# Attention and ReLU² layer on one core: the first batch's values are scaled by spread reciprocals instead of P, and the order is searched anew

## The chip, the cores and the metric

One Trainium2 chip, one of its cores. The metric is the device time of one execution in microseconds (us), median of several runs; less is better. The core has TensorE for matmuls (PE in the profile, PEld for its weight loads), VectorE (DVE), ScalarE (ACT), GpSimd (POOL), and SyncE (SP), whose queue issues the DMAs here.

## What is computed

Causal attention of 4 batches, 12 heads, 448 positions and head dimension 64, its output laid out as 1792 rows of 768, then two matrix products with a squared ReLU between them:

```python
scores = scale * np.matmul(q, k.transpose(0, 1, 3, 2))
scores = np.where(mask, -1000000000.0, scores)
scores = scores - np.max(scores, axis=-1, keepdims=True)
attn = np.exp(scores)
attn = attn / (np.sum(attn, axis=-1, keepdims=True) + 1e-09)
attn_out = np.matmul(attn, v)
x = attn_out.transpose(0, 2, 1, 3).reshape(B * S, H * D)
g = np.maximum(x @ w_in, 0.0) ** 2        # w_in 768 x 2048
out = g @ w_out                           # w_out 2048 x 768
```

All inputs and outputs are fp32. q and k are drawn with a spread of 0.8, v with 0.1.

## The kernel before

Most products run on pairs of fp16 halves: a value is scaled by a power of two and split into an upper half (its rounding to fp16) and a lower half (the rest), and a product is the sum of three fp16 matmuls. The attention of the first batch is the exception. It is done in fp32, because it runs at the very start, while the weights are still being loaded, narrowed to fp32 words, measured (gram matmuls, L1044 and L1093) and split into halves.

`early(part)` computes that first batch, part 0 for positions 0 to 255 and part 1 for positions 256 to 447. Six pairs of heads are worked through in each part. For one pair, `scored` loads nothing itself; it

- turns Q and K by TensorE transposes (L863) and copies them back (L650),
- multiplies them into scores (L884), one PSUM bank for each head and row block,
- masks them and takes the row maxima on DVE (L892), and
- takes exponentials on ACT into P, which also gives the row sums (L896).

`applied` then takes the reciprocals of the row sums on DVE (L906, L909), multiplies each of the four blocks of P by them (`scaled`, L642, on ACT, DVE or GpSimd), turns the blocks of P by TensorE transposes (L924), copies them back (L650), multiplies them with V (L940), and writes the two fp16 halves of x, both read from PSUM: the upper by `activation` or `tensor_scalar` (L953), the lower by `scalar_tensor_tensor` (L957).

After the first part, phase "n" runs the two layers of the first batch (first layer L1250 in groups of 18 matmuls, second layer L1268 in groups of 6, both at lines that later batches share), while the second half of the weights is still being prepared. The second batch's attention begins with transposes at L718 and scores at L773 and L742. The later batches follow, attention of one beside the layers of another; the last block's first layer is a seven-product scheme (L1357, L1472, L1480).

What sets the order: every operation goes into a plan with the engines that may run it, a cost on each, what it reads and writes, and a due time. The due time is a line of the table `PR` (a start and a step for each phase) plus an offset for each kind of operation; another set of entries biases the choice of engine. `Plan.order` goes through the operations with its own clock and puts them on each engine in order of due time among those that are ready by that clock. The result is one fixed instruction order for each engine, and the chip runs each engine's instructions in it, waiting on semaphores.

## Time and profile before

| | |
|---|---|
| median of 3 runs (lowest to highest) | 628.33 us (627.64 to 629.38) |
| the profiled execution: time, span of its instructions | 626.06 us, 624.3 us |
| granted TensorE clock, mean | 0.999 |
| busy share PE, PEld, DVE, ACT, POOL | 96%, 71%, 80%, 74%, 9% |

The profile shows one execution. "Busy" is the time in which at least one instruction of an engine runs. An idle time is put down to what released the waiting instruction. Matmuls overlap in PE's pipeline, so PE's busy time holds some time in which it only waits for a matmul to drain. POOL does almost nothing in the first 160 us.

### The profile page before, as it was taken

What the parts mean: (1) busy time and instruction counts of PE and PEld (TensorE: products, weight loads), DVE (VectorE), ACT (ScalarE), POOL (GpSimd) and SP (SyncE); (2) the same over time, 40 slices, a digit from 0 to 9 for tenths busy, and PEclk for the clock granted to TensorE, in tenths of its full rate; (3) what the DMA queues carried; (4) which work ended last, traced back from release to release, by engine and by line L of the source; (5) the groups of instructions that cost most, each with busy time, mean ns of one, the idle gap of its engine ahead of it and who ended that gap; (6) DMA issues with size and microseconds to landing.
All of it is one profiled execution on the core that took longest, in us unless ns stands there. A gap on an engine that the chain in (4) does not pass through costs nothing.

```text
span 624.3 us, 14273 instructions
## 1 busy us (share of the span) xinstructions
PE 597.0 (96%) x5178; PEld 440.8 (71%) x5178; DVE 501.6 (80%) x1506; ACT 462.0 (74%) x1332; POOL 53.1 (9%) x93
## 2 busy tenths in 40 slices
PE   6788999989999999999999999999999999899997
PEld 4555778878656577886677767887768776687664
DVE  3899999999776899888899889688996999984100
ACT  4989999888998689868999789898647175584000
POOL 0000000000366000000000224132000000000000
PEclk9999999999999999999999999999999999999999
DMA  9974574665657967928997787865500000000100
GB/s 215 351 225 121 169 264 168 227 205 152 145 140 183 208 121 175 168 66 162 214 220 153 136 207 174 165 122 118 132 29 3 27 11 4 1 2 13 39 26 25
DMA packets 190342, 82.52 MB, mean 132 GB/s; under 512 B 177728, under 2 KB 185152, under 8 KB 190272
## 3 DMA queue, kind: packets, MB, share of 16 engines
q1 hardware_dynamic: 190272, 81.62, 53.1%
q8 instruction: 40, 0.66, 0.4%
q14 instruction: 30, 0.25, 0.1%
HBM read 47.19 MB, written 5.51 MB: 84 GB/s over the span
## 4 chain that ended last, share of the span: by engine, by line
PE 59%; DVE 24%; ACT 9%; DMA 5%; issue 2%; SPq 0%; ACTq 0%; DVEq 0%
PE bank L1268 28%; PE bank L1250 15%; PE bank L1472 5%; PE bank L802 4%; PE bank L759 4%; DVE pq L1357 3%; DMA vn<-in_v_dram 3%; DVE wi L1007 2%; DVE bank L892 2%; DVE wi L1004 2%; DVE g L487 1%; DVE wi L1001 1%; PE bank L773 1%; ACT wo L479 1%; DVE bank L742 1%
## 5 line engine op out<-in xcount | busy, mean ns | idle before, releaser
L1268 PE MATMUL bank<-wo,g 128*128 128x384 f16 x1056 | 183.4, 326 | 1.4 <-DVE ob L1285 0.7
L1250 PE MATMUL bank<-xt,wi 128*128 128x256 f16 (+1 forms) x1728 | 168.9, 255 | 1.7 <-ACT r L1213 1.5
L1250 PEld LDWEIGHTS <-wi 128*128 128x128 f16 x1728 | 144.3, 98 | 19.7 <-issue 3.6
L1268 PEld LDWEIGHTS <-g 128*128 128x128 f16 x1056 | 101.5, 98 | 64.4 <-issue 3.0
L746 ACT ACTIVATE pq<-bank,nm 112x112 f32<-112x112 f32 (+3 forms) x144 | 69.8, 493 | 8.4 <-DVE nm L742 7.2
L479 ACT ACTIVATE psrc<-pq,nm 112x336 f16<-112x336 f32 (+3 forms) x144 | 65.9, 526 | 3.7 <-DMA pt<-psrc 1.8
L492 DVE SCALAR_TENSOR_TENSOR psrc<-pq,nm,psrc 112x336 f16<-112x336 f32 (+3 forms) x120 | 59.8, 528 | 3.4 <-ACT psrc L479 2.7
L1285 DVE SCALAR_TENSOR_TENSOR ob<-bank,fac,ob 128x384 f32<-128x384 f32 x26 | 16.0, 614 | 47.5 <-PE bank L1268 47.5
L742 DVE CUSTOM_DVE_ANT_0 bank<-bank,mask,sc 112x112 f32<-112x112 f32 (+3 forms) x96 | 46.2, 512 | 8.1 <-PE bank L759 3.7
L1280 ACT ACTIVATE ob<-bank,fac 128x384 f32<-128x384 f32 x26 | 15.0, 575 | 47.5 <-PE bank L1268 43.8
L487 DVE TENSOR_TENSOR g<-g,g 128x256 f16<-128x256 f32 (+1 forms) x96 | 38.7, 419 | 10.5 <-ACT g L479 10.2
L1220 ACT ACTIVATE g<-r 128x256 f32<-128x256 f32 (+1 forms) x96 | 34.7, 377 | 8.8 <-DVE r L1215 4.0
L479 ACT ACTIVATE g<-g 128x256 f16<-128x256 f32 (+1 forms) x96 | 35.6, 393 | 0.6
L1472 PEld LDWEIGHTS <-wi 128*128 128x128 f16 x288 | 28.2, 98 | 7.2 <-issue 3.4
L759 PE MATMUL bank<-qk 128*112 128x112 f16 (+3 forms) x192 | 31.5, 284 | 0.0
L802 PE MATMUL bank<-pt,vp 112*64 112x224 f16 (+3 forms) x504 | 30.9, 268 | 0.0
L802 PEld LDWEIGHTS <-vp 112*64 112x64 f16 x504 | 23.5, 109 | 10.2 <-issue 6.0
L746 ACT ACTIVATION_READ_ACCUMULATOR pq<-bank,nm 112x1 f32 x144 | 29.2, 203 | 0.0
L495 POOL TENSOR_SCALAR raw<-raw,sc 112x512 f32<-112x512 f32 x12 | 10.1, 846 | 199.3 <-ACT qs L479 199.3
L495 POOL TENSOR_SCALAR pq<-pq,nm 112x112 f32<-112x112 f32 (+1 forms) x24 | 11.2, 467 | 168.1 <-ACT psrc L479 167.0
L759 PEld LDWEIGHTS <-qk 128*112 128x112 f16 x192 | 21.3, 130 | 5.2
L892 DVE CUSTOM_DVE_ANT_0 bank<-bank,mask 128x128 f32<-128x128 f32 (+3 forms) x48 | 21.6, 488 | 3.3 <-PE bank L884 2.9
(195 smaller groups left out, 1125.1 us busy)
## 6 DMA issues: line engine op xcount, KB each, us to landing
raw<-in_moe_w_out_dram SPq DMA_DIRECT2D x8, 768.0 KB, 5.4
xt<-in_moe_w_out_dram SPq DMA_DIRECT2D x8, 768.0 KB, 4.3
xt<-in_moe_w_in_dram SPq DMA_DIRECT2D x11, 512.0 KB, 4.7
out_dram<-ob SPq DMA_DIRECT2D x26, 192.0 KB, 2.0
raw<-in_moe_w_in_dram SPq DMA_DIRECT2D x9, 512.0 KB, 5.5
vn<-in_v_dram SPq DMA_DIRECT2D x18, 224.0 KB, 2.7
raw<-in_v_dram SPq DMA_DIRECT2D x18, 224.0 KB, 3.2
raw<-in_q_dram SPq DMA_DIRECT2D x12, 224.0 KB, 3.2
```

The source lines that it names most:

```text
L479: nc.scalar.activation(out=o, in_=i, func=ACTF.Copy, scale=s)
L487: return plan.add({"dve": dve_ns(n), "pool": pool2_ns(n)}, lambda e: engines[e].tensor_tensor(out=out(), in0=in_(), in1=top(), op=ALU.subt ...
L492: nc.vector.scalar_tensor_tensor(out=out(), in0=in_(), scalar=scale(), in1=top(), op0=ALU.mult, op1=ALU.subtract)
L742: one("dve", dve_ns(w, 1, 2 if F16S[b] else 1) - 10, lambda e: nc.vector.tensor_tensor_reduce(out=s.ap[0:P, 0:w], in0=s.ap[0:P, 0:w], in1= ...
L746: one("act", act_ns(w, True, 1, True), lambda e: nc.scalar.activation(out=p32[j].ap[0:P, b0 * P:b0 * P + w], in_=s.ap[0:P, 0:w], func=ACTF ...
L759: nc.tensor.matmul(out=s.ap[0:P, 0:(c + 1) * P], lhsT=qT.ap[:, j * NCH + c, :], rhs=kT.ap[:, a:a + c + 1, :].rearrange("p a t -> p (a t)") ...
L802: nc.tensor.matmul(out=pv.ap[j * D:(j + 1) * D, ca * P:t1], lhsT=vp.ap[:, hv, vb:vb + D], rhs=pT[j].ap[0:P, hp * ns + x:hp * ns + x + w, : ...
L892: one("dve", dve_ns(w, 1, 1) - 10, lambda e, c=c, j=j, w=w, ss=ss, nm=nm: nc.vector.tensor_tensor_reduce(out=ss[j].ap[0:M, 0:w], in0=ss[j] ...
L1220: nc.scalar.activation(out=g32.ap[:, 0:n], in_=r.ap[:, 0:n], func=ACTF.Square)
L1250: nc.tensor.matmul(out=h.ap[:, 0:n], lhsT=wi_hl(ci, hw)[:, ms], rhs=x[:, kd, hx, off:off + n], start=(kd == 0 and hw == 0 and hx == 0), st ...
L1268: nc.tensor.matmul(out=o.ap[:, 0:HALF], lhsT=gsl(kf, hg, tt * 128, (tt + 1) * 128), rhs=wo_hl(kf, hw)[:, hh * HALF:(hh + 1) * HALF], start ...
L1472: nc.tensor.matmul(out=ps.ap[:, 0:n], lhsT=A[0](f, kd, hw)[:, ms], rhs=B[0](kd, hx), start=(kd == 0 and hw == 0 and hx == 0), stop=(kd == ...
```

## The change

P is no longer multiplied by the reciprocals. TensorE spreads them instead: four small fp32 matmuls for each pair, with the reciprocals of one row block, read 64 times over, as the weights and the identity as the moving operand, write the reciprocal of each position's row sum into all 64 rows of its head, in the same PSUM bank as the values (columns 256 on). A copy brings them to SBUF; then DVE multiplies the values by them and by the power of two of V into an fp32 tile, the upper half is a plain copy of that tile, and the lower half the tile less the upper half. The space is that of P, whose blocks have been turned by then. The transposes of P wait only for the exponentials now; the reciprocals are needed when the values are multiplied.

```diff
             for j in range(2):
                 due = (phase, 2 * pr + j, "P")
-                for c in range(2):
-                    w = T0 + (c + 1) * M
-                    blk = lambda c=c, j=j, w=w, p32=p32: p32[j].ap[0:M, at[c]:at[c] + w]
-                    scaled(w, blk, blk, lambda c=c, j=j: rr(2 * j + c, 2 * j + c + 1), [(p32[j], c), (nm, "r")], [(p32[j], c)], due)
...
+                for c in range(2):
+                    for j in range(2):
+                        nc.tensor.matmul(
+                            out=pv.ap[j * D:(j + 1) * D, 256 + c * M:256 + (c + 1) * M],
+                            lhsT=rr(2 * j + c, 2 * j + c + 1).to_broadcast([M, D]), rhs=ident[0:M, 0:M],
+                            start=True, stop=True)
...
-            one("pe", (mm32_ns(256) + mm32_ns(128) if part == 0 else 3 * mm32_ns(192) + mm32_ns(96)) + 95, values,
-                [k_ for z in range(part + 1) for k_ in early_keys(2, z, pr)] + [(p_, x) for p_ in pT for x in range(part + 1)],
+            one("pe", (mm32_ns(256) + mm32_ns(128) if part == 0 else 3 * mm32_ns(192) + mm32_ns(96)) + 95 + 2 * mm32_ns(M), values,
+                [(nm, "r")] + [k_ for z in range(part + 1) for k_ in early_keys(2, z, pr)] + [(p_, x) for p_ in pT for x in range(part + 1)],
                 [pv], (phase, 2 * pr + 1, "val"), tiled=True)
...
-            plan.add({"act": act_ns(N, True, 1), "dve": dve_ns(N, 1, 1)}, lambda e, xs=xs, pv=pv:
-                     nc.scalar.activation(out=xs[:, 0], in_=pv.ap[:, 0:N], func=ACTF.Copy, scale=v_up(slot)) if e == "act"
...
-            one("dve", dve_ns(N, 1, 1), lambda e, xs=xs, pv=pv: nc.vector.scalar_tensor_tensor(
-                out=xs[:, 1], in0=pv.ap[:, 0:N], scalar=v_up(slot), in1=xs[:, 0], op0=ALU.mult, op1=ALU.subtract),
-                [pv, ("vup", slot)] + xk, xk, due)
+            y = lambda p32=p32: p32[0].ap[:, 0:N]
+            yk = [(p32[0], 0), (p32[0], 1)]
+            br = lambda p32=p32: p32[1].ap[:, 0:N]
+            bk = [(p32[1], 0), (p32[1], 1)]
+            copy(N, br, lambda pv=pv: pv.ap[:, 256:256 + N], [pv], bk, due)
+            one("dve", dve_ns(N, 1, 1), lambda e, y=y, pv=pv, br=br: nc.vector.scalar_tensor_tensor(
+                out=y(), in0=pv.ap[:, 0:N], scalar=v_up(slot), in1=br(), op0=ALU.mult, op1=ALU.mult),
+                [pv, ("vup", slot)] + bk, yk, due)
+            plan.add({"act": act_ns(N), "dve": dve_ns(N, 2)}, lambda e, xs=xs, y=y:
+                     nc.scalar.activation(out=xs[:, 0], in_=y(), func=ACTF.Copy) if e == "act"
+                     else nc.vector.tensor_copy(out=xs[:, 0], in_=y()), yk, xk, due, "top", True)
+            one("dve", dve_ns(N), lambda e, xs=xs, y=y: nc.vector.tensor_tensor(
+                out=xs[:, 1], in0=y(), in1=xs[:, 0], op=ALU.subtract), yk + xk, xk, due, port=True)
```

All numbers of the table `PR` are replaced as well, for instance:

```diff
-    "B1": -4624022, "B2": -750857, "B3": -6169730, "E0": -10980905, "ER": 294079, "F0": -3639158, "FR": 662526,
+    "B1": -4626895, "B2": -1030135, "B3": -5959485, "E0": -11215955, "ER": 274558, "F0": -4013644, "FR": 598546,
```

What that does to the order, in three places. Line numbers of the changed kernel are 1 higher than before up to the edit in `applied`, 3 less at the transposes of P (L924 becomes L921), and 3 to 8 higher behind them (L940 becomes L943, L1250 becomes L1258). All 48 multiplications of P stood on ACT, and all 12 new copies (L651) and upper halves (L964) stand there too.

ACT at the first two pairs, before: exponentials (L896), the multiplications of P (L642), copies of transposes (L650).

```order
L896 ACTIVATE pq,sm<-bank_107,nm 128x128
L896 ACTIVATE pq,sm<-bank_111,nm 128x128
L642 ACTIVATE pq<-pq,nm 128x128
L642 ACTIVATE pq<-pq,nm 128x256
L642 ACTIVATE pq<-pq,nm 128x128
L642 ACTIVATE pq<-pq,nm 128x256
L896 ACTIVATE pq,sm<-bank_115,nm 128x256
L650 ACTIVATE pt<-bank_127 128x384
L650 ACTIVATE pt<-bank_123 128x384
L896 ACTIVATE pq,sm<-bank_119,nm 128x256
```

The same place in the change, up to the first upper half (L964):

```order
L897 ACTIVATE pq,sm<-bank_107,nm 128x128
L651 ACTIVATE pt<-bank_127 128x384
L651 ACTIVATE pt<-bank_123 128x384
L897 ACTIVATE pq,sm<-bank_111,nm 128x128
L651 ACTIVATE wo<-bank_127 128x2x2x128
L897 ACTIVATE pq,sm<-bank_115,nm 128x256
L897 ACTIVATE pq,sm<-bank_119,nm 128x256
L651 ACTIVATE pq<-bank_103 128x256
L651 ACTIVATE pt<-bank_123 128x384
L964 ACTIVATE xt_142<-pq 128x256
```

The four multiplications between the exponentials of the second pair are gone, and the copy of the spread reciprocals (from bank 103) and the upper half come behind those exponentials.

PE at the first two pairs, before: transposes of P (L924), of the next pair's Q and K (L863), values (L940), scores (L884).

```order
L924 MATMUL bank_127<-ident,pq 128x128 x3
L924 MATMUL bank_123<-ident,pq 128x128 x3
L863 MATMUL bank_127<-ident,wo 128x128 x4
L940 MATMUL bank_103<-pt,wo 64x256 x2
L940 MATMUL bank_103<-pt,wo 64x128 x2
```

In the change:

```order
L921 MATMUL bank_127<-ident,pq 128x128 x3
L921 MATMUL bank_123<-ident,pq 128x128 x3
L885 MATMUL bank_115<-wo 128x256
L885 MATMUL bank_119<-wo 128x256
L864 MATMUL bank_127<-ident,wo 128x128 x4
L935 MATMUL bank_103<-ident,nm 64x128 x4
L943 MATMUL bank_103<-pt,wo 64x256 x2
L943 MATMUL bank_103<-pt,wo 64x128 x2
```

The four spreading matmuls (L935) stand directly ahead of the values, and the transposes have moved ahead of half of the second pair's scores.

PE just ahead of the first product of the first layer (L1250), before: the last early work there is a values group (L940) and scores (L884) of part 1, then gram matmuls (L1044, left out here) and one group of transposes (L924).

```order
L863 MATMUL bank_115<-ident,wo 128x96 x4
L940 MATMUL bank_103<-pt,wo 64x192 x6
L940 MATMUL bank_103<-pt,wo 64x96 x2
L884 MATMUL bank_107<-wo 96x256
L884 MATMUL bank_111<-wo 96x256
L884 MATMUL bank_107<-wo 96x96
L884 MATMUL bank_111<-wo 96x96
...
L924 MATMUL bank_115<-ident,psrc_145 128x96 x4
...
L1250 LDWEIGHTS wi
L1250 MATMUL bank_123<-xt_142,wi 128x256
```

In the change:

```order
L935 MATMUL bank_103<-ident,nm 64x96 x4
L943 MATMUL bank_103<-pt,wo 64x192 x6
L943 MATMUL bank_103<-pt,wo 64x96 x2
L921 MATMUL bank_115<-ident,psrc_146 128x96 x4
...
L921 MATMUL bank_115<-ident,psrc_146 96x96 x3
...
L1024 MATMUL bank_127<-wi,dg 128x512
L1025 LDWEIGHTS minus
L1025 MATMUL bank_127<-wi,minus 128x512
L921 MATMUL bank_115<-ident,psrc_146 128x96 x4
L1258 LDWEIGHTS wi
L1258 MATMUL bank_123<-xt_142,wi 128x256
```

The values group shown there is that of the second pair of part 1, where before it was that of the first. Over all that stands ahead of the first layer's first product, PE has 75 transposes of P instead of 54, 52 score matmuls instead of 44, 40 value matmuls instead of 32, 40 transposes of Q and K instead of 36, 7 of the rest pairs (L1016, L1017) instead of 6, 56 gram matmuls as before, and 32 of the 48 spreading matmuls. Ahead of the second batch's first transposes (L718) there are 60 second-layer matmuls instead of 30 and 96 gram matmuls of w_out instead of 90; the 576 first-layer matmuls of the first batch are all ahead of them in both. SyncE issues the first two loads of w_in ahead of the last two loads of V's second half instead of behind them. From about 255 us of the profile before to the end, PE's and DVE's orders are the same in both kernels but for a few second-layer groups, and upper halves of later batches (L815 on DVE, L814 on ACT): DVE has one of these where it had eight.

## Rows read from the trace of the kernel before

**Rows 1.** The page, part 1: busy time, share of the span, instructions.

```profile
PE 597.0 (96%) x5178; PEld 440.8 (71%) x5178; DVE 501.6 (80%) x1506; ACT 462.0 (74%) x1332; POOL 53.1 (9%) x93
```

**Rows 2.** Windows: busy us (x instructions): PE, PEld, DVE, ACT, POOL; clock; DMA.

```profile
20.00:62.00 42.00, 34.77 (x280) 22.40 (x279) 41.64 (x150) 39.06 (x116) 0.00 (x0) 1.00 0.70 222
62.00:120.00 58.00, 56.85 (x540) 45.70 (x538) 57.83 (x141) 55.79 (x147) 0.00 (x0) 1.00 0.61 206
120.00:155.00 35.00, 32.49 (x446) 28.87 (x444) 33.58 (x82) 27.05 (x86) 0.00 (x0) 1.00 0.60 187
155.00:255.00 100.00, 97.28 (x831) 66.35 (x829) 80.81 (x278) 87.64 (x258) 25.55 (x54) 1.00 0.73 158
255.00:485.00 230.00, 229.90 (x2058) 173.44 (x2056) 196.09 (x623) 187.78 (x560) 26.21 (x30) 1.00 0.66 139
```

**Rows 3.** Windows, 0 to 125 us, of L642 alone.

```profile
0.00:125.00 125.00, 22.82 (x48) 1.00 0.69 218
```

**Rows 4.** Timeline: start, duration, instruction, [idle before it and its releaser].

```profile
9.32 2.74 SPq L834 DMA_DIRECT2D wo<-in_v_dram  x4
...
13.70 1.49 ACT L642 ACTIVATE pq<-pq,nm 128x128 f32<-128x128 f32 x4
...
14.31 0.74 PEld L924 LDWEIGHTS bank<-ident,pq 128*128 128x128 f32 x4 [0.65 <-ACT pq L642]
...
16.95 0.17 DVE L906 TENSOR_SCALAR nm<-sm 128x4 f32<-128x4 f32 x1 [2.03 <-ACT pq L896]
...
17.68 0.43 DVE L1001 TENSOR_SCALAR wi<-g 128x512 int32<-128x512 int32 x1 [0.35 <-DMA g<-in_moe_w_in_dram]
```

**Rows 5.** Groups by form: count, busy us, mean ns of one, idle before.

```profile
L1213 ACT ACTIVATE r<-bank 128x256 f32<-128x256 f32 x32 | 11.7, 381 | 2.3 <-PE bank L1250 1.4 <-PE bank L759 0.9
...
L953 ACT ACTIVATE xt<-bank,vst 128x256 f16<-128x256 f32 x6 | 3.0, 492 | 0.0
...
L479 ACT ACTIVATE xt<-g 128x256 f16<-128x256 f32 x8 | 3.1, 403 | 0.0
...
L957 DVE SCALAR_TENSOR_TENSOR xt<-bank,vst,xt 128x256 f16<-128x256 f32 x6 | 2.8, 465 | 0.0
...
L487 DVE TENSOR_TENSOR xt<-g,xt 128x256 f16<-128x256 f32 x8 | 3.3, 418 | 0.3 <-ACT xt L479 0.3
...
L953 ACT ACTIVATE xt<-bank,vst 128x192 f16<-128x192 f32 x6 | 2.5, 415 | 0.0
```

**Rows 6.** Timeline of PE: two groups of value matmuls.

```profile
21.26 0.87 PE L940 MATMUL bank<-pt,wo 128*64 128x256 f32 x8
...
98.49 1.36 PE L940 MATMUL bank<-pt,wo 128*64 128x192 f32 x16
```

**Rows 7.** Windows, 0 to 125 us, of L940, L924, L884, L863, L1016, each alone.

```profile
0.00:125.00 125.00, 14.47 (x144) 9.79 (x144) 1.00 0.69 218
0.00:125.00 125.00, 18.00 (x120) 12.30 (x120) 1.00 0.69 218
0.00:125.00 125.00, 19.77 (x144) 12.30 (x144) 1.00 0.69 218
0.00:125.00 125.00, 8.06 (x48) 6.17 (x48) 1.00 0.69 218
0.00:125.00 125.00, 13.02 (x24) 3.60 (x24) 1.00 0.69 218
```

**Rows 8.** Timeline: first layer, first transposes and score of the second batch.

```profile
62.18 2.02 PE L1250 MATMUL bank<-xt,wi 128*128 128x256 f16 x17
...
155.00 0.55 PE L718 MATMUL bank<-ident,raw 112*128 112x112 f32 x4
...
157.58 0.39 DVE L742 CUSTOM_DVE_ANT_0 bank<-bank,mask 112x224 f32<-112x224 f32 x1
```

**Rows 9.** Groups by form: the second layer.

```profile
L1268 PE MATMUL bank<-wo,g 128*128 128x384 f16 x1056 | 183.4, 326 | 1.4 <-DVE ob L1285 0.7 <-ACT ob L1280 0.7
```

**Rows 10.** One line, L815: duration ns least, median, most, and its forms.

```profile
L815 DVE TENSOR_SCALAR xt<-bank x8: 383/385/620, 212.7 to 416.3; 128x224 f16<-128x224 f32 x6, 128x448 f16<-128x448 f32 x2
```

More of the change, by code (lines that the diff above doesn't have):

```diff
@@ L21 @@
 PR = {
[23 rows of a table removed]
-    "a3_x.top@act": 197941, "a3_x.top@dve": -28752, "bias_act": -83251, "bias_dve": 143093, "bias_pool": 391082,
-    "e_P": -2419284, "e_P.copy@act": -116185, "e_P.copy@dve": -257615, "e_P.nrm@act": 43554, "e_P.nrm@dve": -44495,
-    "e_P.nrm@pool": -113534, "e_ld": 3097901, "e_ldv": -577618, "e_qk": -1629399, "e_qk.copy@act": -330266,
-    "e_qk.copy@dve": 29157, "e_sc": 608399, "e_val": 962496, "e_vn": -827646, "e_x": -3735527, "e_x.top@act": -371196,
-    "e_x.top@dve": -104682, "f_P": -2807427, "f_P.hi@act": -172264, "f_P.hi@dve": 76328, "f_P.hi@pool": 52444,
@@ L50 @@
-    "f_P.lo@dve": -101912, "f_P.lo@pool": 231560, "f_ld": 5282351, "f_ldv": 6107769, "f_qk": 809203,
-    "f_qk.copy@act": 90322, "f_qk.copy@dve": 232713, "f_sc": -1641802, "f_v": 4731699, "f_v.hi@act": -230978,
-    "f_v.hi@dve": -69695, "f_v.hi@pool": -262621, "f_v.lo@dve": -313566, "f_v.lo@pool": -35439, "f_val": -3976137,
-    "f_x": -3990488, "f_x.top@act": 60119, "f_x.top@dve": -168259, "m_L1": 270710, "m_L2": 8389967, "m_c": -2126186,
-    "m_fac": -3581548, "m_ghi": -1839995, "m_ghi.hi@act": -94020, "m_ghi.hi@dve": -74831, "m_ghi.hi@pool": -244397,
@@ L70 @@
-    "ws_wn.rest@act": -77109, "ws_wn.rest@dve": -68307, "wt_wn": 429317, "wt_wn.hi@act": -532389,
-    "wt_wn.hi@dve": -126967, "wt_wn.hi@pool": 36583, "wt_wn.lo@dve": 2939, "wt_wn.lo@pool": -144662,
[24 rows of a table added]
+    "bias_dve": 147220, "bias_pool": 417510, "e_P": -3228041, "e_P.copy@act": -79710, "e_P.copy@dve": -197756,
+    "e_P.nrm@act": 56208, "e_P.nrm@dve": -41261, "e_P.nrm@pool": -127797, "e_ld": 3335729, "e_ldv": 59237,
+    "e_qk": -1394984, "e_qk.copy@act": -314076, "e_qk.copy@dve": 65975, "e_sc": 32607, "e_val": 166206,
@@ new lines @@
+    "e_vn": -752230, "e_x": -4100905, "e_x.copy@act": 12990, "e_x.copy@dve": -23433, "e_x.top@act": -425602,
+    "e_x.top@dve": -100117, "f_P": -2440359, "f_P.hi@act": -180793, "f_P.hi@dve": 107654, "f_P.hi@pool": 16747,
+    "f_P.lo@dve": -115438, "f_P.lo@pool": 203638, "f_ld": 4694296, "f_ldv": 6521064, "f_qk": 760648,
+    "f_qk.copy@act": 87076, "f_qk.copy@dve": 175951, "f_sc": -1086257, "f_v": 4529018, "f_v.hi@act": -228200,
+    "f_v.hi@dve": -40130, "f_v.hi@pool": -263358, "f_v.lo@dve": -315216, "f_v.lo@pool": -31973, "f_val": -3169243,
@@ new lines @@
+    "f_x": -3967276, "f_x.top@act": 42427, "f_x.top@dve": -192415, "m_L1": 55822, "m_L2": 8867493, "m_c": -2620431,
+    "m_fac": -3901656, "m_ghi": -1981522, "m_ghi.hi@act": -58280, "m_ghi.hi@dve": -129330, "m_ghi.hi@pool": -241757,
+    "m_glo": 2420794, "m_glo.lo@dve": 39046, "m_glo.lo@pool": -146432, "m_msq": 5493651, "m_ob": 3699853,
+    "m_one": -252538, "m_one.copy@act": -33145, "m_one.copy@dve": -81526, "m_relu": -6126708, "m_relu.@act": 46599,
+    "m_relu.@dve": -282782, "m_relu2": -4405264, "m_relu2.@act": -140779, "m_relu2.@dve": -199795, "m_rsq": -2051566,
@@ L72 @@
+    "wo_wl": 1160985, "wo_wn": 5752373, "wo_wq": -3880316, "ws_wn": -2603821, "ws_wn.hi@act": 66106,
+    "ws_wn.hi@dve": 5259, "ws_wn.hi@pool": -22272, "ws_wn.lo@dve": 28745, "ws_wn.lo@pool": 172188,
+    "ws_wn.rest@act": -36253, "ws_wn.rest@dve": -70134, "wt_wn": -935486, "wt_wn.hi@act": -499643,
+    "wt_wn.hi@dve": -148552, "wt_wn.hi@pool": 87653, "wt_wn.lo@dve": -29882, "wt_wn.lo@pool": -150721,
 }
@@ L932, in applied, with values @@
             pv = n_pv(0)
-            def values(e, pr=pr, pv=pv, pT32=pT32):
+            def values(e, pr=pr, pv=pv, pT32=pT32, rr=rr):
                 a = 0
+                for c in range(2):
[4 more added lines that the diff above has]
+                            start=True, stop=True)
                 for kc, (k0, height) in enumerate(keyc):
```

28 lines of the change are left out of this document (10 added, 18 removed), and 45 rows, old and new, of the table PR.

## Prediction

> **What bounds the kernel now.** I first read the engines' totals [rows 1]: PE is busy 96% of the span, DVE 80%, ACT 74%. Such shares are averages, so next I cut the span into stages [rows 2]. From 255 us PE is busy 229.90 of 230 us and nothing else matters there. The batch that the change touches is computed in the first 125 us, among the loading and splitting of the weights. There three engines are full at once: from 20 to 62 us DVE 41.64 and ACT 39.06 of 42, with PE at 34.77; from 62 to 120 us DVE 57.83, PE 56.85 and ACT 55.79 of 58. So PE has 7.2 us free between 20 and 62 us, 1.2 us in the next stage and 2.5 us from 120 to 155. Those are the places where a different order can give PE time; after that a microsecond of old PE work that was done earlier is a microsecond off the end.
>
> The first pairs show why PE waits early [rows 4]: ACT multiplies P by the reciprocals in four instructions from 13.70 to 15.19 us, the transposes wait 0.65 us for the first of them, and DVE then sits idle for 2.03 us because the exponentials of the next pair stand behind the four on ACT.
>
> **The changes, part by part.**
>
> *Removed from ACT:* all 48 multiplications of P, 22.82 us busy [rows 3].
>
> *Added to ACT:* 12 copies of the spread reciprocals out of PSUM, six of 256 and six of 192 columns. The nearest row is an activation of the same shape from PSUM, 381 ns [rows 5]; for 192 columns I scale it by 415/492, the ratio of the two forms of the old upper half. 6 x 0.381 + 6 x 0.321 = 4.2 us. The upper half itself is now read from SBUF without a pointer scale: 403 in place of 492 ns, 1.0 us less over twelve. ACT loses 22.8 - 4.2 + 1.0 = 19.6 us.
>
> *Added to DVE:* the old lower half (465 ns) becomes a product of the same shape, which I cost alike; a bound either way is the 418 ns of the tensor-tensor row, 0.6 us over twelve. New are twelve subtractions from SBUF, 418 ns and, scaled, 353: 4.6 us. By the first score of the next batch 13 more small instructions on the output scales are also ahead in DVE's order, at the 0.17 us of the small row [rows 4] 2.2 us. DVE thus has 6.8 us more to do before that score, where it is the fullest engine. What covers this: SyncE now issues the first two w_in loads ahead of two V loads, four of which took it 2.74 us, so the narrowing that waited for its load until 17.68 us [rows 4] can start 1.4 us earlier, inside the old 2.03 us wait; DVE's idle 1.4 us from 120 to 155 us [rows 2] is not counted. The score comes 5.4 us later in DVE's own time.
>
> *Added to PE:* four small fp32 matmuls per pair, 48 in all, in the two 64-column halves like the values. A values group of 768 streamed columns takes 0.87 us and one of 1344 takes 1.36 [rows 6], 1.13 and 1.01 ns a column; 512 and 384 new columns make 0.58 and 0.39, so 6 x 0.97 = 5.8 us. Lower bound by the difference of the two groups (0.85 ns a column, no fixed part) 4.6; upper bound by the mean record of these lines (14.47 us for 144 [rows 7], 96 new records) 9.6. I take 5.8, because the new ones stand directly before a values group and have its form; the upper bound would put 1.0 us more into the full stage below.
>
> *Moved:* this is where the gain must come from. Counted in PE's order, ahead of the first product of the first layer there now stand 21 more transposes of P, 8 more score and 8 more value matmuls, 4 more transposes of Q and K and one more pair of weight-rest matmuls. At the mean price of each line [rows 7], 0.150, 0.275, 0.201, 0.168 and 1.08 + 0.23 us, that is 3.15 + 2.2 + 1.6 + 0.7 + 1.3 = 9.0 us of old work (the 0.23 is an estimate for the fp16 one of the rest pair, 512 columns, from 0.174 us for 384 [rows 9]). With it stand 8 of the 12 new groups, 6 x 0.58 + 2 x 0.39 = 4.3 us. So 13.3 us more must fit ahead of the 62.18 us at which the first layer starts now [rows 8].
>
> How much fits? If busy time is taken at its word, 7.2 us, and the first layer starts 6.1 us later. But the 280 matmuls of 20 to 62 us take 124 ns each and the 540 of 62 to 120 us 105 ns [rows 2]: at the latter rate 29.4 us would do, 12.6 us are free and the start slips 0.7 us. The mix of shapes differs, so these are the two ends; I take the middle, 3.4 us.
>
> The Trainium skill ("Perfetto Trace Analysis", section Identifying the Most-Contended Engine) says that matmul busy time is a poor measure of nearness to the peak, and to read the busy share of weight loads instead. Here that share is 53% from 20 to 62 us against 79% after, which agrees that early PE is less full than its 83% looks; by it 10.7 us would be free and the start would slip 2.6 us, a gain of 4.8 in place of 4.0 below.
>
> PE is then ahead by 9.0 - 3.4 = 5.6 us of old work, and 4 of the new groups (4 x 0.39 = 1.6 us) fall into the full stage. Net 4.0 us; the ends are 1.3 and 6.7.
>
> Does DVE let PE keep it? The first transposes of the next batch run at 155.00 and its first score on DVE at 157.58 us [rows 8]. In PE's new order 30 more second-layer matmuls, at 183.4/1056 = 0.174 us [rows 9], and 6 more gram matmuls (0.5 us) stand ahead of these transposes: 5.7 us. DVE's 5.4 us therefore fall beside PE work, and from 155 to 255 us DVE has 19 and ACT 12 us free to catch up [rows 2]. I charge 0.5 us for waits in between.
>
> *Costed at nothing:* seven upper halves of later batches go from DVE (eight at 383 to 620 ns before [rows 10]) to ACT, and a few second-layer groups change places between 380 and 450 us. PE is busy all of that time [rows 2], which hides them; without this cover, 7 x 0.4 = 2.8 us. Otherwise PE's and DVE's orders are the same from 255 us to the end, so what is ahead there stays ahead.
>
> Sum: -4.0 + 0.5 = -3.5 us. The profiled execution took 626.06 us for a span of 624.3; minus 3.5 it is 622.6. It stands 2.3 us below the median of the runs, 628.33, so for the median I forecast **624.8 us**. A measurement of this kernel tells about 0.3% (1.9 us) from no change.
>
> **Rivals.**
>
> *DVE keeps it all (same time).* The subtraction waits for ACT's upper half, which waits for DVE's product, which waits for ACT's copy: four steps where two were. DVE runs in order, and behind each wait stand the narrowings that feed the gram matmuls and the splits. If the 5.4 us are not caught up after 155 us, PE waits for the scores: -4.0 + 5.4 less the 1.4 us idle = 0, about 628.3. For it: DVE at 99% from 20 to 120 us. Against it: its free 19 us after 155. 22%.
>
> *Both full engines simply got more work (slower).* If the front of PE's new order cannot run early, since the transposes of the second half's pairs wait for scores that DVE delivers no sooner than now, the 9.0 us are not gained and the new matmuls come on top: +5.8 for PE, less the 1.4 that DVE gains in its first wait, about +4.4, 632.7. It decides once the first layer starts later than 62.18 + 9.0 - 1.6, about 69.6 us. For it: the removed 19.6 us lie on the engine with most room of the three over the span [rows 1]. Against it: that engine was 93% and 96% busy exactly where it is relieved [rows 2], and the wait behind the four multiplications is in the trace [rows 4]. 18%.
> The Trainium skill (same page and section) states the rule behind this: improve the engine of highest occupancy first. By it a change that takes work from ACT and gives work to PE and DVE costs time; the trace bears this out over the whole span and speaks against it in the one stage concerned.
>
> *More than forecast.* PE's start does not slip and ACT's freed time shortens all the early chains: -6.7 and beyond, 621.6 or less. For it: the low matmul rate from 20 to 62 us. Against: DVE has no free time there. 12%.
>
> *The multiplications were off the path anyway* is the first rival under another name: ACT's relief then shows only as ACT idle time.
>
> **How the numbers follow.** The forecast, -1.9 to -6, has 48%; with the rival beyond it, faster by over 0.3% has 60%, within 0.3% 22%, slower 18%. The range reaches from a gain of 7.8 us (9.0 - 1.6 with no slip, and 0.4 us of shorter first chains, 620.5) to halfway into the slower rival (630.5); about one in ten lies outside on either side. The forecast case alone spans 622 to 626.5.
>
> **What would show it.** Right: no multiplications of P, ACT under 450 us busy, DVE about 503; PE's idle time from 20 to 62 us down from 7.2 to under 3; the first layer between 62 and 66 us; the first transposes of the next batch at 155 to 158 us with five more second-layer groups ahead of them; the same durations from 255 us on, only earlier. Wrong: the first layer after 69 us; DVE idle before its products or subtractions; the new matmuls at 0.2 us or more each; PE idle before the gram matmuls of w_out, or before the scores between 155 and 255 us, that before does not have.

## The result and the profile after

The changed kernel takes 632.32 us (median of 19 runs, 627.72 to 634.95), the kernel before beside it 628.69 (19 runs, 625.79 to 630.58). The ratio is 1.0052 with a 95% interval of 1.004 to 1.0065: slower by some 3.3 us, where 3.5 us less had been forecast. The profiled execution took 630.03 us for a span of 628.3. Differences in microseconds below are (ratio - 1) x 628.6.

The totals first, part 1 of the page, and from its part 2 TensorE's busy tenths and granted clock:

```profile
PE 604.7 (96%) x5274; PEld 448.1 (71%) x5274; DVE 501.9 (80%) x1511; ACT 450.3 (72%) x1303; POOL 52.5 (8%) x93
...
PE   6989999989999999999999999999999999899997
...
PEclk9979999989999999999999999999999999999999
```

Against [rows 1] ACT lost 11.7 us, PE gained 7.7, DVE 0.3. ACT's 450.3 and DVE's 501.9 us are near what the prediction's list asked for (under 450, about 503). PE gained more than the 5.8 us that its new matmuls were costed at, while its idle time over the span fell from 27.3 to 23.6 us: the 4.0 us by which this profiled execution is longer than that of before stand in PE's busy time and not, in sum, in more waiting. New is the last row: in two slices the granted clock is below full. The stages of [rows 2]:

```profile
20.00:62.00 42.00, 38.48 (x322) 26.03 (x321) 40.09 (x139) 32.70 (x98) 0.00 (x0) 0.92 0.63 197
62.00:120.00 58.00, 58.00 (x572) 46.78 (x571) 57.11 (x156) 50.12 (x139) 0.00 (x0) 1.00 0.62 206
120.00:155.00 35.00, 32.59 (x434) 29.57 (x432) 33.68 (x80) 27.09 (x85) 0.00 (x0) 0.95 0.65 222
155.00:255.00 100.00, 97.46 (x828) 65.83 (x827) 82.37 (x275) 84.98 (x252) 24.96 (x54) 1.00 0.69 154
255.00:485.00 230.00, 228.41 (x2050) 172.99 (x2049) 192.42 (x617) 188.32 (x558) 26.18 (x30) 1.00 0.68 139
```

ACT is relieved where it was meant to be, and PE's idle time from 20 to 62 us fell from 7.2 to 3.5 us. But 42 more matmuls ran there, and the clock column says 0.92. The next windows are the same view around the two dips:

```profile
36.60:40.00 3.40, 1.55 (x16) 1.19 (x15) 3.29 (x12) 1.45 (x4) 0.00 (x0) 1.00 0.66 220
40.00:46.80 6.80, 6.37 (x26) 3.58 (x25) 6.02 (x25) 2.39 (x6) 0.00 (x0) 0.50 0.33 102
128.90:132.20 3.30, 1.30 (x13) 0.86 (x10) 3.27 (x17) 1.39 (x4) 0.00 (x0) 1.00 0.98 333
132.20:135.50 3.30, 3.02 (x29) 3.03 (x30) 3.23 (x15) 2.34 (x6) 0.00 (x0) 0.50 0.77 286
```

The granted clock is 0.50, the lower level of 1.2 GHz, for 6.8 us and again for 3.3 us; in the windows just before, TensorE was busy for 1.55 of 3.4 and 1.30 of 3.3 us. In the first lull its timeline shows what it waited for, and VectorE's one row of the same view:

```profile
36.58 0.39 PE L1052 MATMUL bank<-wi 128*128 128x128 bf16 x4
38.24 0.49 PE L1066 MATMUL bank<-vn,ones_f 128*128 128x128 f32 x2 [1.27 <-DMA xt<-in_moe_w_in_dram]
38.57 0.49 PE L864 MATMUL bank<-ident,wo 96*128 96x96 f32 x4
39.65 0.58 PE L864 MATMUL bank<-ident,wo 96*128 96x96 f32 x4 [0.58 <-ACT wo L651]
```

```profile
37.90 0.29 DVE L1062 TENSOR_SCALAR vn<-ident,wst 128x128 f32<-128x128 f32 x1
```

The first transposes of the second half's pairs (L864, 96 rows) stand behind a matmul of the weights' scale (L1066). The row names a load, but that matmul's input `vn` is written on VectorE from 37.90 to 38.19 us, behind narrowings, a product and a subtraction that run there with no gap over 0.1 us. TensorE had run ahead of the old times (the values of the fourth pair ran at 28.0 instead of 31.8 us, those of the sixth at 35.6 instead of 42.5), and here it has run dry. The new matmuls are as cheap as costed:

```profile
24.10 0.66 PE L935 MATMUL bank<-ident,nm 128*64 128x128 f32 x8
24.59 0.82 PE L943 MATMUL bank<-qk,wo 128*64 128x256 f32 x8
...
55.88 0.55 PE L935 MATMUL bank<-ident,nm 96*64 96x96 f32 x8
56.27 0.99 PE L943 MATMUL bank<-pt,wo 128*64 128x192 f32 x10
```

From the start of a spreading group to that of its values it is 0.49 and 0.39 us (0.58 and 0.39 forecast), 5.3 us over twelve pairs. What came of it stands in three rows that answer to [rows 8]: the first layer's first products, the second batch's first transposes, and its first score on DVE.

```profile
69.49 2.13 PE L1258 MATMUL bank<-xt,wi 128*128 128x256 f16 x18
...
162.70 0.58 PE L719 MATMUL bank<-ident,raw 112*128 112x112 f32 x4
...
164.96 0.28 DVE L743 CUSTOM_DVE_ANT_0 bank<-bank,mask 112x112 f32<-112x112 f32 x1
```

They are 7.3, 7.7 and 7.4 us later. To find who held that first score, compare VectorE from 17 us to its own first score, first before, then after (third group of numbers: DVE; fourth: ACT):

```profile
17.00:157.60 140.60, 129.71 (x1301) 100.54 (x1301) 136.98 (x383) 126.44 (x360) 0.00 (x0) 1.00 0.63 207
```

```profile
17.00:165.00 148.00, 141.98 (x1425) 110.58 (x1422) 142.45 (x407) 118.08 (x345) 0.00 (x0) 0.97 0.64 206
```

DVE has 5.5 us more to do and 1.9 us more idle time: together the 7.4 us. TensorE's second layer, moved ahead of the score in the new order, covers most of this until about 206 us, where a given second-layer matmul runs at the same time as before. What it does not cover is 2.2 us: one group of values and one of scores of the second batch stand ahead of that matmul before, and behind it after.

```profile
203.34 0.62 PE L802 MATMUL bank<-pt,vp 112*64 112x224 f16 x12
...
204.97 1.57 PE L773 MATMUL bank<-raw 64*112 64x336 f32 x8
```

```profile
207.87 0.63 PE L803 MATMUL bank<-pt,vp 112*64 112x224 f16 x12 [0.28 <-DVE xt L819]
208.42 1.57 PE L774 MATMUL bank<-raw 64*112 64x336 f32 x8
```

Then PE waits for the second batch's attention. These are its waits from 205 to 336 us (in total, times, longest), before and after:

```profile
PE bank L773 <- ACT raw L650: 1.8, 2, 1.3
```

```profile
PE bank L803 <- DMA pt<-psrc: 1.9, 3, 0.8
PE bank L774 <- ACT raw L651: 0.5, 1, 0.5
PE bank L760 <- ACT pq L747: 0.5, 1, 0.5
PE bank L557 <- ACT pq L747: 0.4, 1, 0.4
PE bank L803 <- DVE xt L819: 0.3, 1, 0.3
```

They come to 3.6 us where they were 1.8. At 330 us the same matmuls are 4.4 us late, which the 2.2 us and the 1.8 us of longer waits make up but for 0.4, and at the end they are 4.0 us late.

### The profile page after: what moved, and what is told of

The parts are those of the page before. It is cut to its first block, busy times and chain, and to the rows that moved or that the text cites. A ratio compares the mean times of both kernels' runs of the same rounds, so it can differ in the third digit from the quotient of the medians.

```text
span 628.3 us, 14437 instructions
## 1 busy us (share of the span) xinstructions
PE 604.7 (96%) x5274; PEld 448.1 (71%) x5274; DVE 501.9 (80%) x1511; ACT 450.3 (72%) x1303; POOL 52.5 (8%) x93
## 4 chain that ended last, share of the span: by engine, by line
PE 47%; DVE 7%; DMA 3%; ACT 2%; issue 1%; SPq 0%; DVEq 0%
PE bank L1276 23%; PE bank L1258 13%; PE bank L1480 5%; PE bank L803 3%; DVE pq L1365 3%; PE bank L760 3%; DMA pt<-psrc 2%; DMA raw<-in_q_dram 1%; ACT pq L747 1%; DVE raw L488 1%; DVE pq L1488 0%; DVE g L488 0%; DVE psrc L488 0%; ACT g L480 0%; DVE bank L743 0%
## 5 line engine op out<-in xcount | busy, mean ns | idle before, releaser
L1258 PE MATMUL bank<-xt,wi 128*128 128x256 f16 (+1 forms) x1728 | 169.7, 256 | 0.4 <-DVE xt L1185 0.4
L1258 PEld LDWEIGHTS <-wi 128*128 128x128 f16 x1728 | 145.5, 99 | 17.7 <-issue 2.2
```

Of the source, the lines that this page charges most:

```text
L1258: nc.tensor.matmul(out=h.ap[:, 0:n], lhsT=wi_hl(ci, hw)[:, ms], rhs=x[:, kd, hx, off:off + n], start=(kd == 0 and hw == 0 and hx == 0), st ...
```

## The experiments

Three theories were set against each other: **the work** (subtractions on VectorE and spreading matmuls, in a stage that VectorE holds), **the clock** (10 us at 1.2 GHz), and **the order** (the new table is worse, the operations are harmless). Every experiment but the first two keeps the order of its parent, before or after, instruction by instruction, so that only the named work differs.

**Code and table apart (e1_code, e2_table).** The numbers `PR` of one kernel in the code of the other.

> The changed code with the old table of numbers, so that the order is planned anew from the old due times. Theory of the order (the new table leaves TensorE dry at 36 to 40 us and so costs the time): 628 to 629 us, no later than before, and no stretch at 1.2 GHz. Theory of the work (the added subtractions on VectorE and spreading matmuls cost it, whatever the order): 632 us or more, as in the changed kernel.

> The old code with the new table. Theory of the order: slower than before by 2 to 4 us (631 to 633), with a stretch at 1.2 GHz near 40 us. Theory of the work: within 1 us of before (628 to 630), since neither the subtractions nor the spreading matmuls are in it.

New code with the old table: 645.05 us, ratio 1.026 [1.0235, 1.0285]. Old code with the new table: 640.23, 1.0188 [1.0162, 1.0213]. The second misses what either theory expected, and the first, though above the 632 us of the theory of the work, lies 13 us beyond the changed kernel: each table fits its own code only, and the other's costs 12 to 13 us. So for the new code the new table is the better of the two, and a mixture says nothing on the operations. From here on orders were kept.

**The lulls filled (e3_fill).** In the changed kernel:

```diff
@@ behind the weights' gram matmuls at 36.58 us
+                if i == 5:
+                    for _ in range(8):
+                        nc.tensor.matmul(out=bank[4][:, 0:480], lhsT=ones_b, rhs=mask, start=True, stop=True)
@@ behind the sum of squares at 128.9 us
...
+            if phase == "n" and n == 128:
+                for _ in range(6):
+                    nc.tensor.matmul(out=bank[1][:, 0:480], lhsT=ones_b, rhs=mask, start=True, stop=True)
```

> The changed kernel with its order kept, and 8 matmuls of 480 columns that nobody reads at 37 us and 6 at 129 us, where TensorE waits. Theory of the clock (10.2 us at 1.2 GHz delay all that follows): no stretch at 1.2 GHz, first layer 2 to 4 us earlier than 69.5 us, and 628 to 630 us in all. Theory of VectorE (the second batch's attention comes late by VectorE's work, and the clock falls in slack): the clock stays up, but 631.5 to 632.5 us as before the edit.

630.17 us, 1.0031 [1.0014, 1.0047]: 1.3 us less than the changed kernel. The windows answer to those above:

```profile
36.60:40.00 3.40, 3.28 (x28) 2.10 (x24) 3.29 (x11) 0.96 (x4) 0.00 (x0) 1.00 0.68 202
40.00:46.80 6.80, 4.91 (x29) 2.51 (x29) 6.64 (x27) 3.82 (x10) 0.00 (x0) 1.00 0.38 128
128.90:132.20 3.30, 2.22 (x28) 1.80 (x28) 3.23 (x21) 1.04 (x4) 0.00 (x0) 1.00 1.03 415
132.20:135.50 3.30, 2.26 (x41) 2.14 (x39) 3.27 (x12) 2.67 (x6) 0.00 (x0) 1.00 0.41 123
```

With matmuls that nobody reads in the lulls, the granted clock stays at 2.4 GHz, and all 12 executions have a mean of 0.999 or 1.000 (19 of the changed kernel: 0.985 to 0.997). The first layer came only 0.7 us earlier, where 2 to 4 had been expected, and the first score 1.0 us earlier, at 163.94 us. The clock is a part of the loss, some 1.3 of 3.3 us (this difference is uncertain by as much), and not the whole.

**The subtractions left out (e4_nosub), and put on GpSimd (e5_poolsub).** In the changed kernel:

```diff
@@ e4_nosub (and a memset of the lower halves on GpSimd at the start)
-            one("dve", dve_ns(N), lambda e, xs=xs, y=y: nc.vector.tensor_tensor(
-                out=xs[:, 1], in0=y(), in1=xs[:, 0], op=ALU.subtract), yk + xk, xk, due, port=True)
+            one("dve", dve_ns(N), lambda e: None, yk + xk, xk, due, port=True)
@@ e5_poolsub
-            one("dve", dve_ns(N), lambda e, xs=xs, y=y: nc.vector.tensor_tensor(
+            one("dve", dve_ns(N), lambda e, xs=xs, y=y: nc.gpsimd.tensor_tensor(
```

> The changed kernel with its order kept, without the 12 subtractions of the first batch's lower halves (the halves are zero, set once at the start by GpSimd, so the result lacks their part). Theory of VectorE: 4.6 us less on it before the second batch, first score of the second batch 3 to 5 us earlier than 165.0 us, and 628 to 630 us in all. Theory of the clock: both stretches at 1.2 GHz stay and so does the time, 631 to 632.5 us.

> The changed kernel with its order kept, the 12 subtractions on GpSimd in place of VectorE. Theory of VectorE (the second batch's attention starts late against TensorE's other work and costs it waits between 205 and 380 us): first score of the second batch 2 to 4 us earlier than 165.0 us, 629 to 631 us in all. Rival (the port that GpSimd and VectorE share takes the gain back, or the subtractions never were on the path): first score within 1 us of 165.0 us and 632 us or more.

Left out: 630.90 us, 1.0028 [1.0008, 1.0048], 1.5 us less than the changed kernel. The first score came 3.6 us earlier, of the 4.6 us taken away, but not all of that is VectorE's: against the expectation, the clock did not fall in this profiled execution.

```profile
20.00:62.00 42.00, 38.38 (x339) 26.07 (x339) 40.40 (x136) 33.85 (x102) 0.00 (x0) 1.00 0.69 221
...
120.00:155.00 35.00, 31.49 (x426) 27.52 (x424) 34.04 (x80) 27.25 (x86) 0.00 (x0) 1.00 0.63 213
```

A clock that stays up had moved the score by 1.0 us in e3, so VectorE's own part is some 2.6 us (an estimate from these two runs). It holds that score, and the run does not part its work from the clock in the total: the mean clocks of its 12 executions lie between 0.986 and 1.000. On GpSimd: 633.38, 1.0078 [1.005, 1.0106], no gain, as the rival expected. Two groups show one reason (busy us, mean ns of one):

```profile
L966 POOL TENSOR_TENSOR xt<-psrc,xt 128x192 f16<-128x192 f32 (+1 forms) x6 | 11.9, 1984 | 35.7 <-ACT xt L964 35.7
L966 POOL TENSOR_TENSOR xt<-pq,xt 128x256 f16<-128x256 f32 (+1 forms) x6 | 6.0, 1000 | 58.3 <-ACT xt L964 58.3
```

A subtraction that takes VectorE 0.38 us takes GpSimd 0.55 to 1.2 us by its records, but for one of 7.9 us, which makes the mean of 1984 ns. The first score moved by 0.1 us. Whether GpSimd and VectorE hinder each other here was not separated.

**One cost at a time, in the old order (e6_twice, e7_nonorm, e8_spread).** In the kernel before:

```diff
@@ e6_twice
-            one("dve", dve_ns(N, 1, 1), lambda e, xs=xs, pv=pv: nc.vector.scalar_tensor_tensor(
-                out=xs[:, 1], in0=pv.ap[:, 0:N], scalar=v_up(slot), in1=xs[:, 0], op0=ALU.mult, op1=ALU.subtract),
+            one("dve", dve_ns(N, 1, 1), lambda e, xs=xs, pv=pv: [nc.vector.scalar_tensor_tensor(
+                out=xs[:, 1], in0=pv.ap[:, 0:N], scalar=v_up(slot), in1=xs[:, 0], op0=ALU.mult, op1=ALU.subtract) for _ in range(2)],
@@ e7_nonorm
-                    scaled(w, blk, blk, lambda c=c, j=j: rr(2 * j + c, 2 * j + c + 1), [(p32[j], c), (nm, "r")], [(p32[j], c)], due)
+                    plan.add({"act": act_ns(w, False, 1), "dve": dve_ns(w, 2, 1), "pool": pool_ns(w, 1)},
+                             lambda e: None, [(p32[j], c), (nm, "r")], [(p32[j], c)], due, "nrm", True)
@@ e8_spread, ahead of the values' matmuls
+                for c in range(2):
+                    for j in range(2):
+                        nc.tensor.matmul(
+                            out=pv.ap[j * D:(j + 1) * D, 256 + c * M:256 + (c + 1) * M],
+                            lhsT=rr(2 * j + c, 2 * j + c + 1).to_broadcast([M, D]), rhs=ident[0:M, 0:M],
+                            start=True, stop=True)
```

> The kernel before with its order kept, each of the 12 operations that write the first batch's lower halves done twice on VectorE (5.6 us more of it, nothing else). Theory of VectorE: first score of the second batch 4 to 6 us later than 157.6 us, TensorE waits for attention between 205 and 380 us, 630.5 to 632.5 us. Rival (VectorE has room for it, the new order is what costs the time): first score under 2 us later and 628 to 629.5 us.

> The kernel before with its order kept, without the 48 multiplications of P by the reciprocals (22.8 us of ScalarE and nothing put in their place, so the first batch's values are not normalised). Theory of VectorE: ScalarE was not what held the end, gain under 1.5 us (626.5 to 629). Rival (ScalarE held the early stage, as the prediction has it): 624 to 626 us.

> The kernel before with its order kept, with the 48 spreading matmuls added ahead of the values and read by nobody (5.8 us more of TensorE). If TensorE's early idle time (2.4 us at 30 to 45 us, 1.9 us at 45 to 60 us) takes most of it: 628 to 630 us. If it takes none: 633 to 634 us. Theory of VectorE expects the first, 629 to 631 us.

Some 5.4 us more on VectorE: 634.13 us, 1.0081 [1.0064, 1.0099], +5.1 us, above the expected range. The first score moved from 157.58 to

```profile
163.80 0.39 DVE L742 CUSTOM_DVE_ANT_0 bank<-bank,mask 112x224 f32<-112x224 f32 x1
```

and TensorE's lag, 1.2 us at 21 us ahead of the first doubled operation, grows by 5.0 us from there (3.9 at 62, 5.6 at 118, 6.2 at 154). Added VectorE work reaches the end at its full length. The expected waits of TensorE between 205 and 380 us did not appear (1.8 us from 205 to 336 us, as before): in the old order the lag is complete ahead of the second batch. ScalarE's multiplications taken away, 22.8 us by their own rows: 629.18, 0.9993 [0.9973, 1.0014], nothing, and its stages show that VectorE did not notice:

```profile
20.00:62.00 42.00, 33.80 (x279) 22.19 (x280) 41.64 (x150) 30.89 (x92) 0.00 (x0) 1.00 0.71 226
62.00:120.00 58.00, 57.07 (x543) 46.05 (x541) 57.82 (x142) 48.19 (x130) 0.00 (x0) 1.00 0.60 205
```

DVE's 41.64 and 57.82 us are those of [rows 2] to within a hundredth, with ACT at 30.89 for 39.06 and 48.19 for 55.79. Even the wait of 2.03 us that the prediction put down to the multiplications [rows 4] is there without them:

```profile
17.33 0.17 DVE L906 TENSOR_SCALAR nm<-sm 128x4 f32<-128x4 f32 x1 [1.96 <-ACT pq L896]
```

The spreading matmuls alone: 631.88, 1.0047 [1.0025, 1.0069], +3.0 us, between its two cases, first layer at 64.19 and first score at 162.22 us. By the total, TensorE's idle time took about half of them; from 20 to 62 us it fell from 7.2 to 5.7 us.

**The whole edit in the old order (e9_edit).** Copy, product and rounding at the place of the old upper half, the subtraction at that of the old lower half, spreading in front of the values, no multiplication of P.

> The change's operations in the order of the kernel before (spreading matmuls ahead of the values; copy, product and rounding at the place of the old upper half, subtraction at the place of the old lower half, no multiplication of P). Theory of VectorE, by the runs on single parts: 4.5 us of subtractions add some 4 us, the spreading 3 us, the freed ScalarE nothing, so 634 to 638 us, later than the changed kernel: its new order gave a part of it back. Rival (the new order is what lost the time, the operations cost nothing): 627 to 630 us.

638.62 us, 1.0162 [1.0121, 1.0204], +10.2 us, more than the theory's upper end. The first score is at 167.71 us. The new order therefore gives back some 7 of the 10 us (uncertain by almost 3): the search did its part.

**The spreading left out (e11_nospread), and all three costs at once (e14_three).** In the changed kernel; the second joins it with e3 and e4:

```diff
-                for c in range(2):
-                    for j in range(2):
-                        nc.tensor.matmul(
-                            out=pv.ap[j * D:(j + 1) * D, 256 + c * M:256 + (c + 1) * M],
-                            lhsT=rr(2 * j + c, 2 * j + c + 1).to_broadcast([M, D]), rhs=ident[0:M, 0:M],
-                            start=True, stop=True)
...
+        nc.vector.memset(bank[0], 1.0)
```

> The changed kernel with its order kept, without the 48 spreading matmuls (the bank's upper part is set to one at the start, so the values are not normalised). If TensorE's added work is on the path in the new order too: 2 to 4 us less than the changed kernel, 628 to 630.5 us. If VectorE alone holds the early stage: within 1 us of it, 631.5 to 633 us.

> The changed kernel with its order kept, and all three taken away at once: the 12 subtractions, the 48 spreading matmuls, the lulls at 37 and 129 us (filled with matmuls that nobody reads). If the three add up (1.3, 1.5 and 1.8 us as measured one by one): 626.5 to 628.5 us. If they overlap, so that the new order has a loss of its own (the wait for the second batch's attention between 206 and 335 us): 629 to 631 us.

Without spreading: 629.95 us, 1.0023 [1.0004, 1.0043], 1.8 us less than the changed kernel. Its trace does not show where: in the profiled execution, at 631.91 us one of the slowest of the twelve, first layer and first score came later than in the changed kernel, at 70.16 and 166.84 us. Without all three: 627.26, 0.9978 [0.9963, 0.9993], 4.7 us less. One by one they gave 1.3 + 1.5 + 1.8 = 4.6 us. Each difference is uncertain by more than a microsecond, but the sum fits, and PE's waits from 205 to 336 us are down to 2.0 us. The three costs make up the loss, and what is left is a gain of 1.4 us; how the loss divides among them is less sure, since the clock stayed up in e4's profiled execution too. The first score of this faster kernel still comes at 162.23 us, 4.7 us later than before: a late first score is not by itself the loss.

**Relief in the old order (e12_nolow, e13_noadd, e15_both, e16_noprod, e17_two, e18_all).** In the kernel before, in the order of the edits:

```diff
@@ e12_nolow, e15_both, e17_two, e18_all (and a memset of the lower halves on GpSimd at the start)
-            one("dve", dve_ns(N, 1, 1), lambda e, xs=xs, pv=pv: nc.vector.scalar_tensor_tensor(
-                out=xs[:, 1], in0=pv.ap[:, 0:N], scalar=v_up(slot), in1=xs[:, 0], op0=ALU.mult, op1=ALU.subtract),
-                [pv, ("vup", slot)] + xk, xk, due)
+            one("dve", dve_ns(N, 1, 1), lambda e: None, [pv, ("vup", slot)] + xk, xk, due)
@@ e13_noadd (and the reciprocal reads sm in place of nm)
-            one("dve", 69, lambda e: nc.vector.tensor_scalar(
-                out=rr(0, 4), in0=f32(sm, 0, 4), scalar1=1e-9, scalar2=None, op0=ALU.add),
+            one("dve", 69, lambda e: None,
@@ e15_both, e16_noprod, e18_all (first layer)
-                    for hw, hx in ((0, 0), (0, 1), (1, 0)):
+                    for hw, hx in ((0, 0), (0, 1), (1, 0))[:: 2 if phase == "n" else 1]:
```

In e17_two and e18_all the multiplications of P are left out as in e7_nonorm.

> The kernel before with its order kept, without the 12 operations that write the first batch's lower halves (5.3 us of VectorE; the halves are zero, set once at the start by GpSimd). Theory of VectorE: it gives back most of them, 623 to 625.5 us, first score of the second batch 4 to 5 us earlier than 157.6 us. Rival (another engine stands close behind, so that only added work on VectorE counts): 626.5 to 629 us.

> The kernel before with its order kept, without the 12 additions of 1e-9 to row sums that are at least one (2.0 us of VectorE; the result is the same to the bit, since each row sum contains the exponential of zero). Theory of VectorE: 626 to 627.5 us, faster than before. Rival (added work counts, removed work doesn't): 628 to 629.5 us.

> The kernel before with its order kept, the first batch without its lower halves altogether: neither the 12 operations that write them (5.3 us of VectorE) nor the first layer's matmuls that read them (some 15 us of TensorE between 62 and 153 us). Theory that VectorE and TensorE hold 20 to 155 us together: first score of the second batch 4 to 6 us earlier than 157.6 us, 614 to 622 us in all. Rival (VectorE's relief is worth nothing because loads or ScalarE hold it): first score within 2 us of 157.6 us, as without the writing operations alone.

> The kernel before with its order kept, the lower halves written but the first layer's matmuls that read them left out for the first batch (some 15 us of TensorE less, VectorE as before; the result lacks their part). Theory that both engines hold the stage: first score of the second batch within 2 us of 157.6 us, and 618 to 626 us in all. Rival (TensorE alone holds it): first score 6 us or more earlier, and 612 to 617 us.

> The kernel before with its order kept, relieved on VectorE and ScalarE at once: no operations for the first batch's lower halves (5.3 us of VectorE; the halves are zero) and no multiplication of P (22.8 us of ScalarE; the values are not normalised). If ScalarE stands close behind VectorE: first score of the second batch 4 us or more earlier than 157.6 us, and 624 to 626 us in all. If what follows the first score decides: first score about 2 us earlier and 626.5 to 628 us, as without the lower halves alone.

> As the run before it, and without the first layer's matmuls that read the first batch's lower halves (some 15 us of TensorE). If the three engines hold the first stage together: first score 6 us or more earlier than 157.6 us, and under 624 us in all. If VectorE holds it and what follows the first score is full of other work: first score 2 to 4 us earlier, 626 to 629 us.

| relieved | us | ratio, 95% | first score on DVE, us |
|---|---|---|---|
| ScalarE 22.8 (e7) | 629.18 | 0.9993 [0.9973, 1.0014] | 159.13 |
| VectorE 5.3 (e12) | 627.23 | 0.9984 [0.9966, 1.0002] | 155.63 |
| VectorE 2.0 (e13) | 628.04 | 0.9989 [0.9973, 1.0005] | 158.35 |
| TensorE some 15 (e16) | 630.44 | 1.0025 [1.0012, 1.0038] | 159.49 |
| VectorE and TensorE (e15) | 628.29 | 1.0001 [0.9983, 1.002] | 154.75 |
| VectorE and ScalarE (e17) | 624.25 | 0.9942 [0.9921, 0.9963] | 153.53 |
| all three (e18) | 626.12 | 0.997 [0.995, 0.999] | 155.85 |

The first score of a single profile is good to about a microsecond: e16 is already 1.2 us late at 27 us, where its program is still that of before. VectorE alone (e12, e13) fell to the rivals' ranges; e15 and e16 gained nothing, where 612 to 626 us had been expected; and e18 missed the range under 624 us. Two readings stand out. No engine relieved alone gains over 1 us; VectorE and ScalarE together gain 3.6, which is 2.6 more than VectorE alone (uncertain by 1.7). Their windows up to the first score, with VectorE alone relieved and with both:

```profile
17.00:155.60 138.60, 129.96 (x1300) 100.73 (x1300) 134.19 (x370) 126.35 (x360) 0.00 (x0) 1.00 0.64 210
```

```profile
17.00:153.50 136.50, 126.66 (x1291) 99.22 (x1288) 133.19 (x368) 109.23 (x315) 0.00 (x0) 1.00 0.65 214
```

With VectorE relieved alone its idle time rises to 4.4 us (3.6 before); with ScalarE out of the way too it falls to 3.3. And less work on TensorE costs time. In e16 the clock fell once, by stretch:

```profile
124.00:128.00 4.00, 1.97 (x18) 1.51 (x17) 3.32 (x10) 2.23 (x7) 0.00 (x0) 1.00 0.82 277
128.00:132.00 4.00, 3.42 (x25) 2.30 (x23) 3.43 (x16) 3.28 (x9) 0.00 (x0) 0.58 0.72 226
```

Busy for 1.97 of 4 us, and in the next 4 us a mean clock of 0.58. The 12 executions of e18 have a mean clock of 0.989 to 0.997, those of e17 0.997 to 1.000: the same kernel less 15 us of TensorE work is 1.8 us slower. That the clock is the reason was not tried by filling the gaps, and one number speaks against it: the execution of e16 with a mean clock of 1.000 took 630.90 us, above their median of 630.44.

## Why the prediction was wrong

**What ScalarE gives up (19.6 us).** Too large, and wrong as a gain. The copies took 4.3 us (4.2 forecast) and the upper halves 0.75 us less (1.0), but leaving out the multiplications lowers ScalarE's busy time by 17.7 us (e7, 444.3 for 462.0) and not by the 22.8 of their own rows, since neighbouring instructions overlap by some 0.1 us in the records; over the span it lost 11.7, with the seven later upper halves added. The step read "three engines are full at once" and took the relief of one of them as time that PE can use. The wait of 2.03 us in [rows 4] was misread: it is 1.96 us without the multiplications (e7). With nothing put in their place (e7) the multiplications are worth 0.4 us, within the uncertainty. They would be worth about 2.6 us if VectorE were relieved as well (e17 against e12); the change loads VectorE instead.

**What VectorE gets.** The sizes were right: 4.57 us of subtractions (4.6 forecast), 5.5 us more busy time to the first score (6.8), and the first narrowing did start earlier, at 16.35 instead of 17.68 us. But the idle time of DVE grew by 1.9 us, and the score came 7.4 us late where 5.4 was forecast. The charge of 0.5 us for this is the step that failed. It rested on PE's moved work covering the later score and on free time of DVE and ACT behind 155 us. The cover holds up to 206 us but for 2.2 us of work; then the attention that starts 7.4 us late does not catch up, and PE's waits for it between 205 and 336 us grow by 1.8 us. In the old order 5.4 us of such work cost 5.1 (e6); in the new one the subtractions cost some 1.5 (e4).

**What TensorE gets.** 5.3 us for the groups against 5.8: right. That 13.3 us fit ahead of the first layer with a slip of 3.4 us failed: it started 7.3 us later, at 69.49 us, all but the 69.6 us at which the prediction's slower rival decides. Even with the three costs away it starts at 67.05 us in the one profile (e14), 4.9 us late. The early free time of 7.2 us was real. It lay in waits, by the profile of before 5.2 us for copies on ScalarE and 1.9 us for VectorE; the costliest of each:

```profile
PE bank L884 <- ACT wo L650: 3.1, 3, 1.4
PE bank L556 <- DVE s L554: 0.8, 1, 0.8
```

Without the multiplications this idle time is not less but 8.2 us (e7), so the multiplications did not make it. Added matmuls filled a part only (5.7 us are left in e8, 3.5 in the change, at the lower clock). The share of weight loads was also read wrongly, without entering the sum: at the later share 22.40 us of weight loads are 28.4 us of time, and 13.6 us would be free, not 10.7.

**What was not costed at all:** the clock. PE ran ahead, ran dry at 37 us, and was granted 1.2 GHz for 6.8 us just where the moved work was to be done; some 1.3 us in the end (e3).

**What was right.** The moved work does bring something: e9 against the changed kernel shows some 7 us won back by the order, and e14 a net gain of 1.4 us once the three costs are away. The rival "both full engines simply got more work" named the outcome (632.7 us, measured 632.32) and nearly its mechanism; it had 18% because ACT's 93 and 96% were taken for a hold on the stage. That its number came so near is in part luck: it added 5.8 us for PE and took off 1.4 for DVE, and the runs give some 1.8 for the spreading, 1.5 for the subtractions and 1.3 for the clock, less the gain of 1.4. The Trainium skill ("Perfetto Trace Analysis", section Identifying the Most-Contended Engine), whose rule stood behind that rival, has the engine of highest occupancy improved first, TensorE being judged by its share of peak FLOPs and by its weight loads instead of its matmul time. By the weight loads VectorE comes first here (80% of the span before, against 74% of ScalarE and 71% of weight loads): the runs agree that ScalarE was the wrong one to relieve (e7, 0.9993), but VectorE alone, relieved by 5.3 us, gave no clear gain either (e12, 0.9984 [0.9966, 1.0002]).

**Open:** why relief of VectorE alone moves the first score by 2.0 us and not by the 4.5 us that its busy time falls (e12, 497.1 for 501.6) was traced to ScalarE only by the sum (e17), not wait by wait; of the 7 us that the new order gives back, how much belongs to which of its moves was not tried; and the parts of the three costs are each about as large as their uncertainty.

## What to carry to other kernels

Before a change that takes work from one engine and gives some to another, test both halves alone in the old order: leave the work out (e7, nothing) and add the new work idly (e6 and e8, 5.1 and 3.0 us). These three runs would have told the direction, though not the size, since a new order wins a part back (3.3 us were lost in the end). In this stage, where three in-order engines are some 90 to 97% busy, work added to VectorE or TensorE counted, and work removed counted only when it went from VectorE and ScalarE together. No version was found here that beats both kernels and computes the same.

## What the runs showed of the hardware

TensorE's granted clock is a cost of its own. It fell to 1.2 GHz for 6.8 and 3.3 us after stretches in which the engine was busy for 1.55 of 3.4 and 1.30 of 3.3 us, and matmuls that nobody reads, 8 and 6 of 480 columns, kept it at 2.4 GHz and made the kernel some 1.3 us faster. The reverse was seen too: some 15 us of real matmuls taken out made one kernel 1.6 us and another 1.8 us slower, with a clock of 0.58 for 4 us in the first; whether the clock is the reason there was not tried.
